# Decode block on one Trainium2 core: how the late chunk of the down projection is loaded, and where the passes wait

## Chip, cores, metric

One core of one Trainium2 chip runs the whole program. The metric is device time in microseconds, the median of several runs. All data are float32.

## What is computed

A decode step for 8 tokens of width 1024: layer norm, attention with 32 query heads over the last 1024 positions of a cache with 4 key/value heads, output projection and residual; then layer norm, a gated feed-forward of width 3584 and residual.

```python
h = x + attention(layernorm(x), k_cache, v_cache, wq, wo)
n = layernorm(h)
out = h + (gelu(n @ w_gate) * (n @ w_up)) @ w_down      # (8,1024) @ (1024,3584), (3584,1024)
```

The weights and the cache window come to 111 MB, and each is used once.

## The kernel before, in words

**Passes.** The work is seven passes over one PE loop body (`products`, L479): 0 query projection, 1 scores, 2 attention times V, 3 output projection (`WO`), 4 and 5 gate and up columns (`GU0`, `GU1`), 6 the down projection (`DN`). A pass has a side a on buffer `buf[0]` and a side b on `buf[1]`; pass 6 has side a only. A side is eight steps of four matmuls (the profile counts two records for each), whose 32-row results stand in the four quarters of the partitions of `ob`. A full side's load is 8192 KB.

**Waits.** Every place at which PE may have to wait is a name in a fixed order (`pe_order`, L118): for side a of pass k the steps 0 (`a{k}`), CUTS[1] (`a{k}m`) and CUTS[2] (`a{k}l`), with CUTS = (0, 4, 7, 8). `need` (L294 to L419) says which semaphores stand behind a name. GpSimd goes through the names in order (L450 to L457), waits for what a name needs (L455) or for nothing (L457), and counts `go` up by one; PE waits for `go` (L462) and counts it down. So PE learns of a landed load through GpSimd.

**Loads.** SP issues all loads, in order, through `move` (L108): the sides of passes 0 to 4 whole, those of pass 5 in halves of 4096 KB (L187 on), each as soon as PE has left the buffer. Pass 6 has the rows of w_down in pieces: 8 chunks of 128 rows came along with pass 5, 16 chunks are its eight steps (three loads of 4096, 3072 and 1024 KB by CUTS, L194, into `buf[0]`), and four late chunks go to `buf[1]`, free when side b of pass 5 is done. The first late chunk, `singles[0]` of 512 KB (128 rows of 4 KB), is loaded in three pieces of 32, 88 and 8 rows (ROWCUTS, L202 and L203); two more singles of 512 KB and two end blocks of 256 KB follow (L208 and L214). Behind them SP issues 15 `tag` loads (L219) of 15, 14, ... 1 rows with some 100 bytes each, whose data nothing uses; SP waits for them at L441, after it has issued its half of the store.

**The tail on PE.** Steps 0 to 3, 4 to 6 and 7 of pass 6 wait for the three main loads. In two places of pass 6 and one of pass 5 PE repeats an earlier matmul on `fin` (AGAIN, `repeat_residual`, L475; without use for the result). Then come the late chunks: `singles[0]` with two matmuls into quarters 0 and 2 of `ob[0]` (L530), the singles into `fin` (L524), the fold of the sums `d1` that DVE adds up (L426), and the two end blocks (L541), each followed by an ACT copy (L430) and its half of the store, one issued by SP and one by ACT.

Side a of pass 5 starts on its first half as soon as that lands; the second half is awaited at step 4 (L416). In pass 6 step 0 awaits the first main load and ACT's copy `first_ok`, step 4 the second load and ACT's `late_ok` (L417, L418; both copies spread the activations over `st[0]`, L379).

Of the kernel before, what the change touches and what calls it, by code (L numbers as in the profile page):

```python
# [8 lines left out]
P = 128  # L9
B = 8  # L10
D = 1024
# [5 lines left out]
NQ = 4  # L17
CP = 32 // B
QW = D // NQ
N = 512  # L20
# [4 lines left out]
STEPS = 8  # L25
LOAD = STEPS * NQ * N
PASSES = 7
WO, GU0, GU1, DN = 3, 4, 5, 6
CUTS = (0, 4, 7, STEPS)
LAST = DF // P - 1  # L30
EARLY = 8
ENDS = (128, 128)
SINGLE = 3
ROWCUTS = (0, 32, 120, P)
TAGS = 15
AGAIN = (((0, DN, 2), (STEPS // 2, DN, 2)), ((STEPS // 2, GU1, 4),))


class Flow:
# [57 lines left out]
    def run(self, engine, make, *waits, mark=True):  # L97
        ins = self.start(engine, make, waits)
        if not mark:
            return None  # L100
        self.done[engine] += 1
        ins.then_inc(self.own[engine], 1)
        self.tell(engine, self.own[engine], self.done[engine])
        return self.own[engine], self.done[engine]

    def move(self, name, out, src, *waits, engine="sync"):
        s = self.sem(name)
        self.start(engine, lambda e: e.dma_start(out, src), waits).then_inc(s, 16)  # L108
        self.tell(engine, s, 16)
        return s, 16  # L110
# [19 lines left out]
    return out  # L130


def decode_block(nc, x, w, dn, single, ends, outs):
    fl = Flow(nc)
    run, move = fl.run, fl.move
    scale = DH ** -0.5
# [2 lines left out]
    need = {}  # L139
# [30 lines left out]
    ob = [bank(f"o{i}", 2 * N) for i in range(2)]  # L170
# [3 lines left out]
    go = fl.sem("go")  # L174
# [23 lines left out]
    for i in range(SINGLE):  # L198
        t = buf[1][:, i * D:(i + 1) * D]
        if i == 0:  # L200
            here = fl.sem("ws0")
            for a, b in zip(ROWCUTS, ROWCUTS[1:]):  # L202
                fl.start("sync", lambda e: e.dma_start(t[a:b], single[i][a:b]), [pe(f"b{GU1}")]).then_inc(  # L203
                    here, 16)
            here = here, 16 * (len(ROWCUTS) - 1)
        else:
            here = move(f"ws{i}", t, single[i])
        singles.append((t, here))  # L208
    blocks = []
    c0 = 0  # L210
    for i, (n, src) in enumerate(zip(ENDS, ends)):
        a = SINGLE * D + NQ * c0
        t = buf[1][:, a:a + NQ * n]
        blocks.append((n, t, move(f"we{i}", t, src)))  # L214
        c0 += n
# [71 lines left out]
    st_ok = [(t,) for t in tokens_in([pe("t")])]  # L287
    tt_free = st_ok[0]
    o_free = [(), ()]
# [81 lines left out]
    at = sb("at", P, DF // P, 32)  # L371
    ge, g0, u0, u1 = (sb(n, P, N) for n in ("ge", "g0", "u0", "u1"))
    lent = [t.rearrange("p (i r m) -> p i r m", i=STEPS, r=NQ)[:, :, NQ - 1, :] for t in st]
    wide = st[0].rearrange("p (i c m) -> p i c m", i=STEPS, c=2)

    def widen(i0, i1, *ready):

        src = at[:, EARLY + 2 * i0:EARLY + 2 * i1].rearrange("p (i e) m -> p i (e m)", e=2)
        return run("scalar", lambda e: e.copy(  # L379
            wide[:, i0:i1], src.unsqueeze(2).to_broadcast([P, i1 - i0, 2, 64])), *ready)  # L380
# [40 lines left out]

# [10 lines left out]
    mark = sb("mark", 1, 1)  # L432
# [14 lines left out]
        nc.sync.wait_ge(s, val).then_inc(s, -val)  # L447


    for name in [n for kind, n in order if kind == "wait"]:  # L450
        left = fl.missing("gpsimd", need.get(name, []))
        for s, v in left[:-1]:
            nc.gpsimd.wait_ge(s, v)
        if left:
            nc.gpsimd.wait_ge(*left[-1]).then_inc(go, 1)  # L455
        else:
            nc.gpsimd.sem_inc(go, 1)  # L457
    assert set(need) <= {n for kind, n in order if kind == "wait"}, need


# [35 lines left out]
    with nc.Fori(-1, PASSES, engines=[mybir.EngineType.PE]) as it:  # L496
        with nc.tensor.If(it >= 0):
            wait()
            turn(xs[1])
            products(0, CUTS)  # L500
            with nc.tensor.If(it < DN):
# [3 lines left out]
                with nc.tensor.If(it == WO):  # L505
                    wait()
                    for ch in range(2):
                        ins = nc.tensor.matmul(
                            fin[0:ROWS, ch * N:(ch + 1) * N], to_rows[:, ch, :], y_sb,
                            start=True, stop=True)  # L510
                    marked(ins)
                    wait()
                    for ch in range(2):
# [3 lines left out]
                            start=True, stop=True)  # L517
                    marked(ins)

    def add(lhs, rhs, *waits, start=False):  # L520

        for d_ps, a, b in halves:
            for j in range(NQ):
                run("tensor", lambda e: e.matmul(  # L524
                    d_ps[32 * j:32 * j + 32, :], lhs(j), rhs(j)[:, a:b], start=start, stop=False),
                    *waits, mark=False)

    (t, here), *rest = singles
    for ch in range(2):
        tok = run("tensor", lambda e: e.matmul(  # L530
            ob[0][64 * ch:64 * ch + 32, N:2 * N], at[:, LAST - SINGLE, :], t[:, ch * N:(ch + 1) * N],
            start=False, stop=True, skip_group_check=True), here, at_ok, mark=(ch == 1))
    assert tok == odd_done
    for i, (t, here) in enumerate(rest):
        add(lambda j: at[:, LAST - SINGLE + 1 + i, :], lambda j: t[:, j * QW:(j + 1) * QW], here,
            start=(i == 0))
        if i == 0:
            add(lambda j: add2[:, j // 2, :], lambda j: d1[:, (j % 2) * QW:(j % 2) * QW + QW], d1_ok)
    for (n, t, here), (d_ps, a, b) in zip(blocks, halves):
        for j in range(NQ):  # L540
            run("tensor", lambda e: e.matmul(  # L541
                d_ps[32 * j:32 * j + 32, :], at[:, LAST, :], t[:, j * n:(j + 1) * n],
                start=False, stop=True), here, mark=(j == NQ - 1))
# [65 lines left out]
```

## Time and profile before

| | |
|---|---|
| median of 3 runs | 268.08 us (267.64 to 270.53) |
| the profiled execution | 267.8 us, its span 266.2 us |
| mean granted TensorE clock | 0.833 |
| read from HBM | 111.19 MB, 418 GB/s over the span |
| PE busy | 145.5 us (55%) |
| VectorE, ScalarE, GpSimd busy | 28.6, 28.5, 5.3 us |

How to read it. The span runs from the first to the last instruction of the program; the program's own time is somewhat longer. A row of the timeline gives the start, the length, engine and line, the operation with its tiles, the count and, in brackets, how long the engine had been idle and what ended that. "SPq", "PEq" and "POOLq" are the sequencers' own instructions (issues of loads, waits). A row by stage has each engine's busy time (and its instructions) within that stretch, then the granted clock, the busy share of the 16 DMA engines (a packet is put down to the stretch in which it starts, so 1.03 can occur) and what they moved. In the DMA answer for a stretch, "packets" counts rows of data and the 4-byte notices at a load's end ("under 512 B").

### The profile page before, as it was taken

How to read it: one execution, taken by the hardware profiler on the slowest of the kernel's cores; microseconds unless marked ns; L12 is line 12 of the kernel's file. 1: busy time of each engine (PE TensorE's matmuls, PEld its weight loads, DVE VectorE, ACT ScalarE, POOL GpSimd, SP SyncE). 2: the span in 40 equal slices, each digit the busy share in tenths (PEclk: the TensorE clock that was granted, in tenths of full speed). 3: DMA queues.
4: the chain of work that ended last, by engine and by line, in shares of the span. 5: the costliest groups of instructions: out<-in, count | busy, mean ns of one | idle time of the engine just before them, and what ended most of it. 6: DMA issues, size and time to landing. Idle time of an engine off the chain costs nothing. (4 is left out here: it accounts for less than half of the span.)

```text
span 266.2 us, 2425 instructions
## 1 busy us (share of the span) xinstructions
PE 145.5 (55%) x1028; PEld 50.3 (19%) x1028; DVE 28.6 (11%) x47; ACT 28.5 (11%) x49; POOL 5.3 (2%) x11
## 2 busy tenths in 40 slices
PE   0023924815716727518519609638829564886784
PEld 0021211201211222102102202122202221322222
DVE  0310020100100100500500101430100201002101
ACT  1030000020030030010010000033300102002000
POOL 8000000000000000000000000000000000000000
PEclk9999995975975956966965968975977999799979
DMA  8997999799979997999799979997999999999994
GB/s 318 468 473 325 473 463 473 325 473 463 473 325 473 463 473 325 473 463 473 325 473 463 473 335 463 463 473 335 463 394 468 394 473 394 473 394 435 420 274 164
DMA packets 3735, 111.38 MB, mean 418 GB/s; under 512 B 651, under 2 KB 907, under 8 KB 1555
## 3 DMA queue, kind: packets, MB, share of 16 engines
q1 hardware_dynamic: 3571, 111.23, 98.0%
q10 hardware_dynamic: 160, 0.10, 0.1%
q8 instruction: 2, 0.03, 0.0%
q14 instruction: 2, 0.02, 0.0%
HBM read 111.19 MB, written 0.13 MB: 418 GB/s over the span
## 5 line engine op out<-in xcount | busy, mean ns | idle before, releaser
L489 PE MATMUL o<-w,st 128*32 128x512 f32 x832 | 116.3, 717 | 79.0 <-PEq L462 47.4
L489 PEld LDWEIGHTS o<-w,st 128*32 128x32 f32 x832 | 32.8, 129 | 154.9 <-issue 154.9
L469 PE MATMUL tt<-ident,zeros 128*128 128x128 f32 x104 | 16.5, 311 | 35.8 <-PEq L462 35.8
L469 PEld LDWEIGHTS tt<-ident,zeros 128*128 128x128 f32 x104 | 13.3, 159 | 46.2 <-issue 46.2
L475 PE MATMUL fin<-zeros,spread 128*32 128x512 f32 x16 | 7.4, 594 | 0.0
L331 DVE SCALAR_TENSOR_TENSOR av<-o,rtot,own 128x512 f32<-128x512 f32 x4 | 3.0, 750 | 31.3 <-PE o L489 31.3
L314 DVE TENSOR_REDUCE nmax<-o 128x1 f32<-128x1024 f32 x2 | 2.5, 1225 | 35.3 <-PE o L489 35.3
L341 ACT COPY st<-tt 128x512 f32<-128x512 f32 x4 | 2.1, 588 | 35.4 <-PE tt L469 35.4
L316 ACT ACTIVATE zeros<-o,nmax 128x1024 f32<-128x1024 f32 x2 | 2.2, 1114 | 33.6 <-DVE nmax L314 33.6
L356 DVE TENSOR_TENSOR y_sb<-o,y_sb 128x512 f32<-128x512 f32 x3 | 2.1, 692 | 34.2 <-PE o L489 34.2
L296 DVE SCALAR_TENSOR_TENSOR zeros<-o,tq 128x512 f32<-128x512 f32 x2 | 1.4, 692 | 36.1 <-PE o L489 36.1
L399 DVE TENSOR_TENSOR u<-o,u 128x512 f32<-128x512 f32 x2 | 1.4, 692 | 35.1 <-PE o L489 35.1
L390 DVE TENSOR_TENSOR g<-o,g 128x512 f32<-128x512 f32 x2 | 1.4, 692 | 24.6 <-PE o L489 24.6
L295 ACT ACTIVATE tq<-o 128x512 f32<-128x512 f32 x2 | 1.2, 597 | 24.0 <-PE o L489 24.0
L334 DVE TENSOR_REDUCE zeros<-av 128x128 f32<-128x1024 f32 x2 | 3.7, 1871 | 0.1
L398 ACT COPY u<-o 128x512 f32<-128x512 f32 x2 | 1.2, 586 | 21.0 <-PE o L489 21.0
L363 ACT COPY zeros<-fin 32x512 f32<-32x512 f32 x1 | 0.6, 574 | 26.4 <-PE fin L514 26.4
L227 POOL MEMSET zeros<- 128x3712 f32 x1 | 3.2, 3191 | 0.0
L263 ACT ACT_TABLE_LOAD x2 | 2.6, 1283 | 2.9 <-POOL ident L224 2.9
L279 ACT COPY st<-tt 128x1024 f32<-128x1024 f32 x2 | 2.0, 1012 | 7.7 <-PE tt L469 7.7
L405 ACT COPY at<-tt 128x512 f32<-128x512 f32 (+1 forms) x2 | 1.1, 532 | 16.0 <-PE tt L469 16.0
L475 PEld LDWEIGHTS fin<-zeros,spread 128*32 128x32 f32 x16 | 1.7, 110 | 4.5 <-issue 4.5
(57 smaller groups left out, 40.9 us busy)
## 6 DMA issues: line engine op xcount, KB each, us to landing
w<-ends SPq DMA_DIRECT2D x5, 4096.0 KB, 25.3
w<-ends SPq DMA_DIRECT2D x1, 3072.0 KB, 32.2
w<-ends SPq DMA_DIRECT2D x1, 1024.0 KB, 36.2
w<-ends SPq DMA_DIRECT2D x2, 512.0 KB, 18.7
w<-ends SPq DMA_DIRECT2D x2, 256.0 KB, 19.5
w<-ends SPq DMA_DIRECT2D x1, 352.0 KB
w<-w SPq DMA_DIRECT2D x10, 29.5
w<-ends SPq DMA_DIRECT2D x1, 128.0 KB
```

The costliest lines, as they stand in the source:

```text
L227: clear = run("gpsimd", lambda e: e.memset(zeros, 0.0))
L263: tok = run("scalar", lambda e: e.activation(sd, ve, AF.Sqrt), tok)
L279: a = run("scalar", lambda e: e.copy(st[0].rearrange("p (c r b) -> p c r b", c=NC, b=B), xt.unsqueeze(2).to_broadcast([P, NC, P // B, B])) ...
L314: tok = run("vector", lambda e: e.tensor_reduce(out=nmax, in_=ob[s], axis=AX.X, op=ALU.max, negate=True), pe(f"{h}1"))
L316: tok = run("scalar", lambda e: e.activation(xs[s], ob[s], AF.Exp, bias=nmax, accum_out=tot), tok)
L331: tok = run("vector", lambda e: e.scalar_tensor_tensor(av[:, i], o3, rtot, own.unsqueeze(2).to_broadcast([P, HB, DH]), op0=ALU.mult, op1=A ...
L334: tok = run("vector", lambda e: e.tensor_reduce(out=out, in_=av.rearrange("p i b d -> p d (i b)"), axis=AX.X, op=ALU.add), tok)
L341: tok = run("scalar", lambda e: e.copy(heads[:, g], turned.unsqueeze(2).to_broadcast([P, REP, P // 2 // B, B])), pe(f"t{h}2"))
L356: tok = run("vector", lambda e: e.tensor_add(y_sb, part, y_sb), ready, tok)
L469: ins = nc.tensor.transpose(t8[:, i, :], src[:, i * P:(i + 1) * P], ident)
L475: nc.tensor.matmul(fin[0:32, 0:N], spread.rearrange("p r b -> p (r b)"), h_sb[:, 0:N], start=True, stop=True)
L489: ins = nc.tensor.matmul(ob[s][32 * r:32 * r + 32, c:c + N], st[s][:, i * P + 32 * r:i * P + 32 * r + 32], buf[s][:, (i * NQ + r) * N:(i * ...
```

## The change

1. The first late chunk is laid out anew on the host. Its columns 0 to 511 stay as 128 rows of 2 KB (`w_odd`, one load through `move`). Its columns 512 to 1023 become 64 rows of 4 KB on partitions 0 to 63 (`w_low`): row p has the half row of partition p and, behind it, that of partition p + 64. Eight loads of eight rows bring them; load j writes partitions p0, p0 + 4, ... p0 + 28 with p0 from OFFSETS. The matmuls on the chunk are three: all 128 rows into quarter 0, and two with 64 rows into quarters 2 and 3 (the fold adds both). For the last one ACT copies the upper 64 partitions of the activations down (`at_low`).
2. CUTS becomes (0, 5, 7, 8): the main loads are 5120, 2048 and 1024 KB, and PE's middle wait stands at step 5. Both halves of pass 5's side a are now awaited at step 0, and `late_ok` at step 0 of pass 6. The second repeat of pass 6 moves to step 5.
3. GpSimd no longer takes a step of its own for a name without needs: the wait before it counts `go` up by as many as follow it.

```diff
-CUTS = (0, 4, 7, STEPS)
+CUTS = (0, 5, 7, STEPS)
-ROWCUTS = (0, 32, 120, P)
+LOW = P // 2
+OFFSETS = (0, 1, 2, 3, 32, 33, 34, 35)
-AGAIN = (((0, DN, 2), (STEPS // 2, DN, 2)), ((STEPS // 2, GU1, 4),))
+AGAIN = (((0, DN, 2), (CUTS[1], DN, 2)), ((STEPS // 2, GU1, 4),))
...
+    w_odd, w_low = buf[1][:, 0:N], buf[1][0:LOW, N:N + D]
+    odd_in = [move("wo0", w_odd, single[0], pe(f"b{GU1}"))]
+    low_in = fl.sem("w_low")
+    for j, p0 in enumerate(OFFSETS):
+        nc.sync.dma_start(w_low[p0:p0 + 29:4], side[j]).then_inc(low_in, 16)
+    odd_in.append((low_in, 16 * len(OFFSETS)))
-        if i == 0:
-            here = fl.sem("ws0")
-            for a, b in zip(ROWCUTS, ROWCUTS[1:]):
-                fl.start("sync", lambda e: e.dma_start(t[a:b], single[i][a:b]), [pe(f"b{GU1}")]).then_inc(
-                    here, 16)
...
-        need[f"a{k}"] = [landed[k, 0][0], *st_ok[0], *o_free[0]]
+        need[f"a{k}"] = [*landed[k, 0], *st_ok[0], *o_free[0]]
...
+            low_ok = run("scalar", lambda e: e.copy(at_low, at[LOW:P, LAST - SINGLE, :]), at_ok)
-    need[f"a{GU1}m"] = [*landed[GU1, 0][1:], res_ok]
-    need[f"a{DN}"] = [landed[DN, 0][0], first_ok, *o_free[0]]
-    need[f"a{DN}m"] = [landed[DN, 0][1], late_ok]
+    need[f"a{GU1}m"] = [res_ok]
+    need[f"a{DN}"] = [landed[DN, 0][0], first_ok, late_ok, *o_free[0]]
+    need[f"a{DN}m"] = [landed[DN, 0][1]]
...
+    steps = []
     for name in [n for kind, n in order if kind == "wait"]:
         left = fl.missing("gpsimd", need.get(name, []))
+        if left or not steps:
+            steps.append([left, 1])
+        else:
+            steps[-1][1] += 1
+    for left, n in steps:
         for s, v in left[:-1]:
             nc.gpsimd.wait_ge(s, v)
-        if left:
-            nc.gpsimd.wait_ge(*left[-1]).then_inc(go, 1)
-        else:
-            nc.gpsimd.sem_inc(go, 1)
+        nc.gpsimd.wait_ge(*left[-1]).then_inc(go, n)
...
-    for ch in range(2):
+    odd = LAST - SINGLE
+    for i, (q, lhs, t) in enumerate((
+            (0, at[:, odd, :], w_odd), (2, at[0:LOW, odd, :], w_low[:, 0:N]),
+            (3, at_low, w_low[:, N:2 * N]))):
         tok = run("tensor", lambda e: e.matmul(
-            ob[0][64 * ch:64 * ch + 32, N:2 * N], at[:, LAST - SINGLE, :], t[:, ch * N:(ch + 1) * N],
-            start=False, stop=True, skip_group_check=True), here, at_ok, mark=(ch == 1))
+            ob[0][32 * q:32 * q + 32, N:2 * N], lhs, t, start=False, stop=True,
+            skip_group_check=True), *odd_in, at_ok, low_ok, mark=(i == 2))
...
+    low = odd[:, 1].reshape(2, LOW, N).transpose(1, 0, 2)
+    parts += [np.stack([low[p0:p0 + 29:4] for p0 in OFFSETS]), odd[:, 0]]
```

More of the change, by code (lines that the diff above doesn't have):

```diff
@@ L130, in pe_order, with decode_block @@
     return out
-def decode_block(nc, x, w, dn, single, ends, outs):
+def decode_block(nc, x, w, dn, side, single, ends, outs):
     fl = Flow(nc)
@@ L196, in decode_block @@
         for i, (a, b) in enumerate(zip(CUTS, CUTS[1:]))]
-    singles = []
-    for i in range(SINGLE):
-        t = buf[1][:, i * D:(i + 1) * D]
-        if i == 0:
-            here = fl.sem("ws0")
-            for a, b in zip(ROWCUTS, ROWCUTS[1:]):
-                fl.start("sync", lambda e: e.dma_start(t[a:b], single[i][a:b]), [pe(f"b{GU1}")]).then_inc(
-                    here, 16)
-            here = here, 16 * (len(ROWCUTS) - 1)
-        else:
-            here = move(f"ws{i}", t, single[i])
-        singles.append((t, here))
+    w_odd, w_low = buf[1][:, 0:N], buf[1][0:LOW, N:N + D]
[4 more added lines that the diff above has]
+    odd_in.append((low_in, 16 * len(OFFSETS)))
+    singles = []
+    for i in range(1, SINGLE):
+        t = buf[1][:, N + i * D:N + (i + 1) * D]
+        singles.append((t, move(f"ws{i}", t, single[i])))
     blocks = []
@@ L211, in decode_block @@
     for i, (n, src) in enumerate(zip(ENDS, ends)):
-        a = SINGLE * D + NQ * c0
+        a = N + SINGLE * D + NQ * c0
         t = buf[1][:, a:a + NQ * n]
@@ L373, in decode_block @@
     lent = [t.rearrange("p (i r m) -> p i r m", i=STEPS, r=NQ)[:, :, NQ - 1, :] for t in st]
+    at_low = sb("at_low", LOW, 32)
     wide = st[0].rearrange("p (i c m) -> p i c m", i=STEPS, c=2)
@@ L447, in decode_block @@
         nc.sync.wait_ge(s, val).then_inc(s, -val)
+    steps = []
     for name in [n for kind, n in order if kind == "wait"]:
         left = fl.missing("gpsimd", need.get(name, []))
+        if left or not steps:
[3 more added lines that the diff above has]
+    for left, n in steps:
         for s, v in left[:-1]:
             nc.gpsimd.wait_ge(s, v)
-        if left:
-            nc.gpsimd.wait_ge(*left[-1]).then_inc(go, 1)
-        else:
-            nc.gpsimd.sem_inc(go, 1)
+        nc.gpsimd.wait_ge(*left[-1]).then_inc(go, n)
     assert set(need) <= {n for kind, n in order if kind == "wait"}, need
@@ L526, in add @@
                     *waits, mark=False)
-    (t, here), *rest = singles
-    for ch in range(2):
+    odd = LAST - SINGLE
+    for i, (q, lhs, t) in enumerate((
+            (0, at[:, odd, :], w_odd), (2, at[0:LOW, odd, :], w_low[:, 0:N]),
+            (3, at_low, w_low[:, N:2 * N]))):
         tok = run("tensor", lambda e: e.matmul(
-            ob[0][64 * ch:64 * ch + 32, N:2 * N], at[:, LAST - SINGLE, :], t[:, ch * N:(ch + 1) * N],
-            start=False, stop=True, skip_group_check=True), here, at_ok, mark=(ch == 1))
+            ob[0][32 * q:32 * q + 32, N:2 * N], lhs, t, start=False, stop=True,
+            skip_group_check=True), *odd_in, at_ok, low_ok, mark=(i == 2))
     assert tok == odd_done
-    for i, (t, here) in enumerate(rest):
-        add(lambda j: at[:, LAST - SINGLE + 1 + i, :], lambda j: t[:, j * QW:(j + 1) * QW], here,
+    for i, (t, here) in enumerate(singles):
+        add(lambda j: at[:, odd + 1 + i, :], lambda j: t[:, j * QW:(j + 1) * QW], here,
             start=(i == 0))
@@ L579 @@
     parts += [main[:, a * NQ:b * NQ] for a, b in zip(CUTS, CUTS[1:])]
-    parts += [down[:, i] for i in range(LAST - SINGLE, LAST)]
+    odd = down[:, LAST - SINGLE]
+    low = odd[:, 1].reshape(2, LOW, N).transpose(1, 0, 2)
+    parts += [np.stack([low[p0:p0 + 29:4] for p0 in OFFSETS]), odd[:, 0]]
+    parts += [down[:, i] for i in range(LAST - SINGLE + 1, LAST)]
     parts += [row[:, :, a:b] for a, b in zip(cuts, cuts[1:])]
@@ L600 @@
     w = [aps["w"][i] for i in range(2 * GU1)] + small[0:4]
-    dn, single, ends = small[4:7], small[7:7 + SINGLE], small[7 + SINGLE:]
-    decode_block(nc, aps["x"], w, dn, single, ends, outs)
+    dn, side, single, ends = small[4:7], small[7], small[8:8 + SINGLE], small[8 + SINGLE:]
+    side = side.rearrange("p n -> (p n)").rearrange("(j r n) -> j r n", j=len(OFFSETS), r=8)
+    decode_block(nc, aps["x"], w, dn, side, single, ends, outs)
     r = run_bass_kernel_spmd(nc, [arrays], core_ids=[0])
```

## The prediction

> **What bounds the kernel now.** I read the page first, then the chain that ended last, then busy time by stage, then the DMA answer for short stretches of the tail, then the timeline of the last 20 us.
>
> ```profile
> span 266.2 us, 2425 instructions
> PE 145.5 (55%) x1028; PEld 50.3 (19%) x1028; DVE 28.6 (11%) x47; ACT 28.5 (11%) x49; POOL 5.3 (2%) x11
> q1 hardware_dynamic: 3571, 111.23, 98.0%
> ...
> 243.35 19.61 DMA w<-ends
> ...
> 263.01 0.47 PE fin L541 x8
> ...
> 263.50 0.27 ACT o_fin L430
> ```
>
> SP's queue keeps the 16 DMA engines taken for 98.0% of the span, and the chain ends with one load of 19.61 us that lands at 262.96 (243.35 + 19.61); then 0.47 us of PE, 0.27 us of ACT and the store follow. So the kernel ends when the last of its loads lands. The program took 267.8 us with this profile, 1.6 us more than its span; the median of the runs shown is 268.08 us, 0.28 more. My sum is a difference of spans, taken off that median.
>
> A busy DMA engine is not a fast one, and the stages show it:
>
> ```profile
> core 0: us, PE busy (x) PEld busy (x) DVE busy (x) ACT busy (x) POOL busy (x), PEclk, DMA share, GB/s
> 237.00:246.80 9.80, 6.54 (x44) 2.34 (x44) 1.39 (x2) 1.71 (x3) 0.00 (x0) 1.00 1.02 440
> 254.10:258.60 4.50, 4.44 (x24) 1.27 (x24) 0.00 (x0) 0.00 (x0) 0.00 (x0) 0.62 1.03 223
> 258.60:263.00 4.40, 3.69 (x71) 1.88 (x68) 0.75 (x2) 0.23 (x1) 0.00 (x0) 1.00 0.80 291
> ```
>
> While the first part of the main down rows is loaded, the engines are full at 440 GB/s. From 254.10 to 258.60 they are just as full (1.03) and move 223. That stretch holds the three row pieces of the late chunk. Had it run at 440, it would have been (1 - 223/440) x 4.50 = 2.2 us shorter. The same in two shorter stretches, the pieces first, then the ordinary 4 KB rows behind them:
>
> ```profile
> DMA packets 151, 0.52 MB, mean 187 GB/s; under 512 B 25, under 2 KB 25, under 8 KB 149
> q1 hardware_dynamic: 151, 0.52, 104.3%
> ...
> DMA packets 182, 0.56 MB, mean 402 GB/s; under 512 B 20, under 2 KB 20, under 8 KB 182
> q1 hardware_dynamic: 182, 0.56, 101.9%
> ```
>
> Between 255.60 and 258.40 a row of some 4 KB holds its engine for 2.80 x 16 x 1.043 / 126 = 0.37 us; between 259.20 and 260.60 one of the same kind takes 1.40 x 16 x 1.019 / 162 = 0.14 us. By engine these are 187/1.043/16 = 11.2 GB/s and 402/1.019/16 = 24.7 GB/s. Row size and busy engines are alike; what differs is which partitions an engine writes. I read it as engines standing in each other's way at the SBUF side: with 88 rows over fewer engines than 16, each takes a block of rows that other engines write too.
>
> **The change part by part.** *The late chunk's loads.* Its 512 KB move as one load of 128 rows of 2 KB (spread as the other full loads) and eight loads of 8 rows of 4 KB, whose rows stand four partitions apart, one row for each of eight engines. So eight engines carry 16 + 32 KB of the chunk, the others 16 KB. To time an engine I need when it begins the third main load:
>
> ```profile
> DMA packets 61, 0.49 MB, mean 410 GB/s; under 512 B 1, under 2 KB 1, under 8 KB 1
> q1 hardware_dynamic: 61, 0.49, 98.3%
> ...
> 254.16 5.54 PE L489 MATMUL o<-w,st 128*32 128x512 f32 x32 [1.98 <-PEq L462]
> ```
>
> Between 252.75 and 253.95, 60 rows of 8 KB (0.49 MB / 60) begin: they are the third main load's. All 16 engines at 440/1.02/16 = 27.0 GB/s would begin 63, so about 15 of them are past the second load at 252.75, yet PE gets that load only at 254.1: one engine is some 1.4 us behind. I put the others at 252.6 (half a row earlier), the late one at 254.0. Each then has, by rates of 27.0 (8 KB rows) and 24.7 (smaller): third main load 64 KB 2.43 us, the 2 KB rows 0.66, its eight 4 KB rows 1.33 (eight engines only), the two single chunks 2.65, the two end blocks 1.33. That is 8.40 us for the eight, 7.07 for the rest. The eight finish at 261.0, with 0.2 for the telling 261.2. The late engine, if it is among the rest, finishes at 254.0 + 7.07 = 261.1. Against 262.96 the last landing is **1.8 us** earlier.
>
> The price of a small load beyond its bytes has no row of its own. Nearest are the fifteen tag loads behind the last block:
>
> ```profile
> SPq L441 <- DMA tag<-w: 2.2, 1, 2.2
> L219 SPq DMA_DIRECT2D tag<-w x15: 252/329/2694, 243.8 to 253.7; - x15
> ...
> 240.84 1.12 SPq L203 DMA_DIRECT2D w<-ends  x3
> 242.01 1.78 SPq L108 DMA_DIRECT2D w<-ends  x4
> 243.83 10.15 SPq L219 DMA_DIRECT2D tag<-w  x15
> 263.13 0.37 SPq L108 DMA_DIRECT2D out<-o_fin  x1
> ```
>
> SP waits for them from 263.50 (263.13 + 0.37) for 2.2 us, to about 265.7: 2.8 us after the last block, 0.19 each. Eight such prices are 1.5 us; below, nothing, and no gain. I take nothing: between 259.20 and 260.60 twenty 4-byte notices passed among 162 rows at 24.7 GB/s. The Trainium skill's page "DMA: Bandwidth & Descriptors" speaks against the change: its "Rules for kernel authors" would have small transfers gathered, since under 64 KB one pays mostly overhead. Its table of measured sizes (0.68 us for 4 KB, 0.95 for 64 KB) would make eight loads cost about 6.4 us as an estimate, and the sum would turn into a loss of some 3 us.
>
> *SP's queue.* Six more issues at 0.37 to 0.45 us (1.12/3, 1.78/4) are 2.2 to 2.7 us; the fifteen tags behind them would end at 254 + 2.7 = 256.7, and should SP be held up again as in the 2.7 us issue above, at 259.4. The store's turn comes at 261.3, so 1.9 us of cover are left; the loads themselves wait behind a full queue.
>
> *Cuts at 5 and 7, the second half of pass 5's load, late copies.* The step 0 wait now covers both halves of that load:
>
> ```profile
> 211.91 3.64 PE L489 MATMUL o<-w,st 128*32 128x512 f32 x32 [1.28 <-PEq L462]
> ...
> 217.74 3.64 PE L489 MATMUL o<-w,st 128*32 128x512 f32 x32 [2.18 <-POOLq L457]
> ...
> 227.44 5.24 PE L489 MATMUL o<-w,st 128*32 128x512 f32 x32 [5.04 <-PEq L462]
> 232.43 3.60 PE L475 MATMUL fin<-zeros,spread 128*32 128x512 f32 x8
> 237.16 3.64 PE L489 MATMUL o<-w,st 128*32 128x512 f32 x32 [1.12 <-PEq L462]
> ...
> 244.15 0.62 ACT L379 COPY st<-at 128x512 f32<-128x512 f32 x1
> ```
>
> The 3.64 us at 211.91 move behind 217.74, so that half ends at 225.0 and its turn in time for the next load at 227.4: nothing. Behind the longer wait GpSimd has only the same pass's later increments, which PE alone awaits. At half clock throughout, the half would end at 232.3, and what follows (5.24 + 3.60 us) at some 241 where PE goes on at 237.16 now: 4 us late. Then the late copies, ready at 244.8 (244.15 + 0.62) and now awaited at step 0 of the last pass, would come at 249, when that step's load lands, and the late chunk would be issued at 245, ten microseconds ahead of its turn. So hidden even then, with little to spare.
>
> In the last pass the first part holds five steps, 1 MB more at 440 GB/s, and lands at 246.8 + 2.4 = 249.2. What PE then has to do, from rows of before:
>
> ```profile
> 246.87 3.64 PE L489 MATMUL o<-w,st 128*32 128x512 f32 x32 [1.43 <-PEq L462]
> 250.30 1.88 PE L475 MATMUL fin<-zeros,spread 128*32 128x512 f32 x4
> 259.49 1.06 PE L530 MATMUL o<-w,at 128*32 128x512 f32 x4
> 260.66 0.69 DVE L426 TENSOR_TENSOR d<-o,d 128x512 f32<-128x512 f32 x1 [9.33 <-PE o L530]
> 261.41 0.64 PE L524 MATMUL fin<-d,add 128*32 128x128 f32 x16 [0.42 <-DVE d L426]
> 261.87 0.62 PE L524 MATMUL fin<-w,at 128*32 128x128 f32 x16
> 262.31 0.40 PE L541 MATMUL fin<-w,at 128*32 128x128 f32 x8
> 263.01 0.43 PE L541 MATMUL fin<-w,at 128*32 128x128 f32 x8 [0.30 <-DMA w<-ends]
> ```
>
> From start to start 32 matmul records take 3.43 us (246.87 to 250.30). Five steps take 4.3, to 253.5; the repeats, moved to step 5, 1.7, to 255.3 (the second part landed at 254.1, so they delay it by 1.1); two steps 1.7, to 257.0; the last 0.9, to 257.9. The chunk is there at 257.2. Three matmuls stand in place of two; the two ran side by side in 1.06 us, and I let the third do so (between 0 and 0.5 us more). The DVE add starts 1.17 later, the fold 0.75, the last single 0.46, the first end block 0.44: 260.7. The last block lands at 261.2, so PE has half a microsecond in hand. The new copy of 64 partitions is one ACT instruction of about 0.6 us at 246 or so, 10 us ahead of its use.
>
> *Fewer GpSimd waits.*
>
> ```profile
> L457 POOLq EVENT_SEMAPHORE  x18: 17/17/17, 24.0 to 217.7; - x18
> ```
>
> Eighteen bare increments of 17 ns go. All stand beside loads that are on their way; worth nothing, 0.3 us (18 x 17 ns) at the very most.
>
> **Sum.** Last landing -1.8 us; PE, SP and GpSimd 0; the 3.2 us from landing to end (262.96 to 266.2) as before. 268.08 - 1.8 = **266.3 us**.
>
> **The rivals.** *PE takes over the end.* The granted clock was 0.62 from 254.10 to 258.60, after PE had idled 1.98 us. Half clock in one stretch of 3.4 us (a half pass of 32 records) costs 1.7 us of work. The first end block's work would start at 262.4, the last one's at 262.8 where before had 263.01: -0.2, **267.9 us**. For it: half a microsecond of slack. Against: the repeats now fill the gap that cooled PE. The Trainium skill's "TensorE: Matmul & The Clock Gate", Part 1, says that the activity window runs freely, so that the place of the drop may vary; no single trace can show that.
>
> *The late engine is among the eight, or stepped rows clash as well.* The page does not tell which engine is late. It would end at 254.0 + 8.40 = 262.4: -0.6, **267.5 us**. For: the eight carry more. Against: before ended with a DMA share of 0.80 from 258.60 on, so several engines had run out early, and those had the two rows only.
>
> *Small loads hold their engines (slower).* If each of the eight costs a fixed time in series, the chunk and all behind it come later. From 1.8/8 = 0.22 us a load the gain is gone; at SP's own issue price, 0.45, it is 8 x 0.45 - 1.8 = 1.8 us lost, **269.9 us**, and from 0.56 over 1%; the far end is a store's whole way, 2.4 us (below), and 17 us lost. For: the tags' 0.19 is close to the turning point. Against: the notices seen above hold nothing up.
>
> *More than the clash goes.* With all rows at 27.0 GB/s the eight have 208 KB, 7.9 us, and end at 260.7: -2.3; if the store, 2.4 us from issue to landing now, also finds the queue free of tags and lands 0.7 earlier, **265.1 us**.
>
> ```profile
> out<-o_fin ACTq DMA_DIRECT2D x1, 64.0 KB, 2.4
> ```
>
> **How the numbers follow.** Forecast 0.60, PE 0.15, late engine or clash 0.10, small loads 0.07, more 0.08. The range 265.2 to 268.4 runs from just above the last rival over 267.9 to a small-load price near the tags' 0.19 with a little PE on top; it leaves out the small-load rival and most of the last one, some 0.15. About 1% (2.7 us) is what a measurement of this kernel can tell from no change. Faster by more needs 265.4: the last rival and a sliver of the forecast, 0.10. Slower by more needs 270.8: most of the small-load rival, 0.05. Within: 0.85.
>
> **What would show it.** Right: 254 to 258 at well over 300 GB/s where 223 stood; 4 KB rows at 0.14 to 0.17 us throughout; the last block's matmuls at about 261.3; PE there waiting for DMA. Wrong: rows still at 0.37 us (clash); the odd chunk's matmuls after 259 with PE idle before them (small loads); the last block's matmuls directly behind other PE work at half clock (PE); an SP issue of tags that reaches past 261.

## The result, and the profile after

| | before | changed |
|---|---|---|
| median | 268.00 us (20 runs, 267.49 to 270.71) | **267.37 us** (20 runs, 265.66 to 268.04) |
| ratio to before, with its 95% interval | | 0.9943 [0.9917, 0.9968] |
| the profiled execution | 267.8 us, span 266.2 | 265.81 us, span 264.5 |

The change is a gain of half a per cent, inside what the forecast called no change, and inside its range. But the median hides the more useful fact. The 20 runs of the changed kernel lie in two groups with nothing between them: seven from 265.66 to 265.95 and thirteen from 267.19 to 268.04. The profiled execution belongs to the first. Disturbed runs are left out of every ratio here.

The page of the changed kernel (span, and the chain that ended last by engine and by line). Line numbers have moved: the products are L493, the repeats L479, the late chunk L536, singles and fold L528, end blocks L547.

```profile
span 264.5 us, 2418 instructions
...
PE 5%; DVE 0%; ACT 0%; issue 0%; DVEq 0%
PE o L493 3%; PE o L536 1%; PE fin L479 1%; PE fin L528 0%; DVE d L427 0%; ACT o_fin L431 0%; PE fin L547 0%; DVE mark L434 0%; DVEq L92 0%
```

The chain no longer has a load in it. It was one load of 19.61 us; now it is PE from the start of the last pass on. Busy time by stage, with the stretch 254.10 to 258.60 that the forecast argued from:

```profile
237.00:249.20 12.20, 8.23 (x44) 2.80 (x44) 1.38 (x2) 1.93 (x4) 0.00 (x0) 0.86 0.94 405
249.20:254.10 4.90, 4.74 (x42) 1.68 (x43) 0.69 (x1) 0.00 (x0) 0.00 (x0) 1.00 0.97 408
254.10:258.60 4.50, 4.50 (x30) 1.24 (x28) 0.00 (x0) 0.00 (x0) 0.00 (x0) 1.00 1.01 396
258.60:261.30 2.70, 2.41 (x41) 1.01 (x44) 0.69 (x2) 0.00 (x0) 0.00 (x0) 1.00 0.55 192
```

396 GB/s stand where 223 stood, at the same full engines, and from 258.60 to 261.30 the engines are already half idle (0.55). The DMA answers for 255.5 to 257.5, where the eight small loads are under way, for the issue of the last end block, and for the store:

```profile
DMA packets 268, 0.82 MB, mean 408 GB/s; under 512 B 66, under 2 KB 66, under 8 KB 267
q1 hardware_dynamic: 268, 0.82, 103.0%
...
w<-ends SPq DMA_DIRECT2D x1, 256.0 KB, 11.3
...
out<-o_fin ACTq DMA_DIRECT2D x1, 64.0 KB, 1.8
```

There are 268 - 66 = 202 rows in 2.0 us, nearly all of 4 KB (0.82 MB / 202): the stepped rows and those of the single chunks behind them. So a 4 KB row takes 2.0 x 16 x 1.03 / 202 = **0.163 us** where it took 0.37. The store took 1.8 us from issue to landing where it took 2.4. The timeline of the end:

```profile
243.00 5.45 SPq L202 DMA_DIRECT2D w<-ends  x8
...
249.36 4.50 PE L493 MATMUL o<-w,st 128*32 128x512 f32 x40 [2.14 <-PEq L466]
...
249.93 0.43 SPq L109 DMA_DIRECT2D w<-ends  x1
250.40 5.65 SPq L218 DMA_DIRECT2D tag<-w  x15
253.65 1.45 PE L479 MATMUL fin<-zeros,spread 128*32 128x512 f32 x3
...
257.94 1.56 PE L536 MATMUL o<-w,at 128*32 128x512 f32 x3
258.89 0.10 PEld L536 LDWEIGHTS o<-w,at 64*32 64x32 f32 x1 [0.84 <-issue]
258.90 0.61 PE L536 MATMUL o<-w,at_low 64*32 64x512 f32 x1
...
260.06 0.69 DVE L427 TENSOR_TENSOR d<-o,d 128x512 f32<-128x512 f32 x1 [6.24 <-PE o L536]
...
261.70 0.62 PE L547 MATMUL fin<-w,at 128*32 128x128 f32 x16
262.69 0.35 ACTq L109 DMA_DIRECT2D out<-o_fin  x1
```

The last end block, issued at 249.93, landed 11.3 us later, at **261.2**. PE reached its 16 matmul records at 261.70, both blocks in one go and with no wait in front: the data had been there for half a microsecond. PE ends the kernel.

### The profile page after: what moved, and what is told of

The parts are those of the page before. It is cut to its first block, busy times and chain, and to the rows that moved or that the text cites. A ratio compares the mean times of both kernels' runs of the same rounds, so it can differ in the third digit from the quotient of the medians.

```text
span 264.5 us, 2418 instructions
## 1 busy us (share of the span) xinstructions
PE 147.1 (56%) x1030; PEld 50.4 (19%) x1030; DVE 28.5 (11%) x47; ACT 28.7 (11%) x50; POOL 5.3 (2%) x11
## 5 line engine op out<-in xcount | busy, mean ns | idle before, releaser
L493 PE MATMUL o<-w,st 128*32 128x512 f32 x832 | 118.0, 725 | 76.5 <-PEq L466 70.1
L493 PEld LDWEIGHTS o<-w,st 128*32 128x32 f32 x832 | 33.0, 130 | 153.0 <-issue 152.9
L479 PE MATMUL fin<-zeros,spread 128*32 128x512 f32 x16 | 7.4, 594 | 0.0
L389 ACT COPY g<-o 128x512 f32<-128x512 f32 x2 | 1.2, 586 | 16.2 <-PE o L493 16.2
## 6 DMA issues: line engine op xcount, KB each, us to landing
w<-ends SPq DMA_DIRECT2D x3, 256.0 KB, 11.3
```

What stands on the lines that cost most here:

```text
L479: nc.tensor.matmul(fin[0:32, 0:N], spread.rearrange("p r b -> p (r b)"), h_sb[:, 0:N], start=True, stop=True)
L493: ins = nc.tensor.matmul(ob[s][32 * r:32 * r + 32, c:c + N], st[s][:, i * P + 32 * r:i * P + 32 * r + 32], buf[s][:, (i * NQ + r) * N:(i * ...
```

## Experiments

**What was to be told apart.** Theory: the new loads bring the last landing from 263.0 to 261.2 and nothing else in the change gains; PE, now last, decides the rest, and the second group of runs is PE at half clock in the last pass. Rivals: the cuts or the GpSimd part bring the gain; the stepped rows are not what ends the clash; small loads have a price that eight of them already pay; the second group has another cause.

**1. The changed kernel again.** No edit.

> The changed kernel once more, unaltered, for its spread and a second profile. Its runs fall in two groups, near 265.8 and near 267.5 us. Theory (PE's clock): the last block has landed at about 261.2 in both groups; in the slower one the main steps of the last pass run at half clock for one stretch and all PE work behind them comes 1.7 us later, so that the last end block's matmuls start near 263.6 with their data long there. Rival (the loads): in the slower group the last block itself lands 1.7 us later, near 263, and PE waits for it.

Measured: 267.39 us median of 12 runs, 0.9962 [0.9944, 0.998]; ten runs lie from 267.11 on, two at 266.44 and 266.63, between the two groups. This time the profile (267.39 us, span 266.1) was of the slower group. Its timeline and the stage 249.20 to 254.10:

```profile
237.29 3.64 PE L493 MATMUL o<-w,st 128*32 128x512 f32 x32 [2.32 <-PEq L466]
...
248.28 0.43 SPq L109 DMA_DIRECT2D w<-ends  x1
249.41 6.07 PE L493 MATMUL o<-w,st 128*32 128x512 f32 x40 [3.84 <-PEq L466]
...
259.58 1.56 PE L536 MATMUL o<-w,at 128*32 128x512 f32 x3
...
263.34 0.62 PE L547 MATMUL fin<-w,at 128*32 128x128 f32 x16
```

```profile
249.20:254.10 4.90, 4.69 (x32) 1.42 (x36) 0.00 (x0) 0.00 (x0) 0.00 (x0) 0.65 0.97 411
...
w<-ends SPq DMA_DIRECT2D x1, 256.0 KB, 12.9
```

The last block landed at 248.28 + 12.9 = 261.2, as before. But the five steps from 249.41 took 6.07 us, not 4.50, at a granted clock of 0.65, not 1.00; everything behind is 1.64 us later (259.58 against 257.94, 263.34 against 261.70), and so is the span (266.1 against 264.5). Both profiles have one stretch of half clock near the end, 3.4 us long by the clock's records. In the first it ran from 237.8 to 241.2, on the half pass before (a mean clock of 0.86 from 237.00 to 249.20), which has time to spare. In the second that half pass ran warm in 3.64 us, PE was done sooner and idled 3.84 us, not 2.14, and the half clock ran from 249.2 to 252.6, in the last pass, where nothing is spare. That the longer idle time brought it there is argued, not shown: experiment 9 has it there after 2.13 us. The forecast took from the Trainium skill ("TensorE: Matmul & The Clock Gate", Part 1) that the activity window runs freely and the place of the drop may vary; these two profiles of one program agree, with 0.65 and 1.00 in the same stage.

**2 to 4. The parts alone.** Kernel before with part 2 alone (cuts and waits); with parts 1 and 3 (loads, GpSimd, the old cuts); with part 3 alone. Of each its first line:

```diff
+CUTS = (0, 5, 7, STEPS)
...
+OFFSETS = (0, 1, 2, 3, 32, 33, 34, 35)
...
+        nc.gpsimd.wait_ge(*left[-1]).then_inc(go, n)
```

> The kernel before with only the cuts at 5 and 7, the waits that go with them and the moved repeat; loads of the late chunk and GpSimd's steps as before. Theory (the loads bring the gain): last landing at 263.0 as before, time 268.0, ratio 1.000. Rival (the cuts bring some of it): ratio below 0.998. PE's slack before the last block was 0.3 us; should the half clock fall on it, up to 0.5 us slower.

> The new layout and loads of the late chunk with the old cuts, waits and repeats (GpSimd's merged steps stay). Theory (loads give, PE takes): the last block lands at about 261.2 as with the full change; the half clock after the idle gap before step 4, as in the profile of before, makes the chunk's matmuls start near 259.4 and the last block's near 263.2: time 267.2 to 267.6, ratio 0.998. Rival (the landing decides): 266.2, ratio 0.993.

> The kernel before with only GpSimd's merged steps. Theory: nothing, ratio 1.000 within the interval, last landing at 263.0. Rival (PE waited for the bare increments on the path that sets the end): 0.1 to 0.3 us faster.

| kernel | median us | ratio, 95% interval |
|---|---|---|
| cuts alone | 268.55 (12 runs) | 1.0002 [0.9982, 1.0022] |
| loads and GpSimd, old cuts | 267.03 (12 runs) | 0.9944 [0.9918, 0.9971] |
| GpSimd alone | 267.81 (10 runs) | 0.9991 [0.9957, 1.0025] |

The chain of the cuts alone, then of GpSimd alone, then the stage of the loads alone:

```profile
243.45 19.95 DMA w<-ends
```

```profile
243.44 19.60 DMA w<-ends
```

```profile
254.10:258.60 4.50, 4.48 (x28) 1.57 (x32) 0.00 (x0) 0.00 (x0) 0.00 (x0) 0.64 1.02 402
```

Without the new loads the last block still lands at 263.4 and 263.0 and ends the kernel. With them the stretch moves 402 GB/s. So the loads bring the whole gain; the cuts and the fewer GpSimd steps bring nothing that can be measured. The loads alone have the two groups as well (four of the 12 runs at 265.9 to 266.1), and in their profile, 267.17 us, the half clock (0.64) fell on 254.10 to 258.60, as expected; their median is a little under the 267.2 to 267.6 expected of it.

**5. PE kept busy where it may cool, and free where it is late.** The repeats at step 5 go, seven are put ahead of side a of pass 5, and four, not two, ahead of the last pass. The repeats are not used by the result.

```diff
-AGAIN = (((0, DN, 2), (CUTS[1], DN, 2)), ((STEPS // 2, GU1, 4),))
+AGAIN = (((0, GU1, 7), (0, DN, 4)), ((STEPS // 2, GU1, 4),))
```

> The change with other repeats: seven more before side a of pass 5, four in place of two before step 0 of the last pass, none at step 5, so that PE has no idle stretch of several us before its last work. Theory (PE's clock): one group, all near 265.8 us, ratio 0.992 to before; granted clock 1.00 from 249 on. Rival (the two groups come from the loads): still two groups, median near 267.4, ratio 0.995 to 0.997.

Measured: 266.15 us median of 8 runs, 0.9921 [0.9896, 0.9946]; of the seven that the ratio counts, six lie at or under 266.43 and one at 267.23. Timeline and landing:

```profile
249.99 0.43 SPq L109 DMA_DIRECT2D w<-ends  x1
...
257.76 1.56 PE L536 MATMUL o<-w,at 128*32 128x512 f32 x3
...
261.52 0.62 PE L547 MATMUL fin<-w,at 128*32 128x128 f32 x16
```

```profile
w<-ends SPq DMA_DIRECT2D x1, 256.0 KB, 11.2
```

The landing is untouched (249.99 + 11.2 = 261.2), and so is the rate while the small loads are under way (408 GB/s from 255.5 to 257.5). PE's end is only 0.18 earlier than in the changed kernel's first profile, and the clock is 1.00 from 249.20 on. The median falls by 1.2 us (267.39 to 266.15), so PE has a part in the second group. But the edit does two things, and it is not shown that the clock is the one that counts: of the later profiles with the same repeats, those of experiments 7, 8 and 9 have half clock (0.65) from 249.20 to 254.10 all the same. Here are the row and the timeline of 9, whose loads are those of this experiment:

```profile
249.20:254.10 4.90, 4.49 (x28) 1.59 (x32) 0.00 (x0) 0.00 (x0) 0.00 (x0) 0.65 0.99 416
...
249.61 8.77 PE L493 MATMUL o<-w,st 128*32 128x512 f32 x64 [2.13 <-PEq L466]
258.17 1.56 PE L536 MATMUL o<-w,at 128*32 128x512 f32 x3
```

PE begins the chunk at 258.17, 0.41 us after 257.76, where the same half clock cost 1.64 us in experiment 1. Without the repeats at step 5 PE's eight steps run through in one go, and most of the half clock is made up before the chunk is there. So at least part of the gain comes from the repeats that went, not from a clock that stayed up.

**6 to 8. What the eight stepped loads avoid, and what they cost.** All three have the repeats of experiment 5, which is what they are compared with (by the ratios, for they ran on another chip and beside other runs of the kernel before: a median of 267.94 us there, 268.05 for experiment 5). 6: the same eight loads, on eight consecutive partitions each. 7: the 64 rows in one load. 8: sixteen loads of eight rows of 2 KB.

```diff
-        nc.sync.dma_start(w_low[p0:p0 + 29:4], side[j]).then_inc(low_in, 16)
+        nc.sync.dma_start(w_low[8 * j:8 * j + 8], side[j]).then_inc(low_in, 16)
...
+    nc.sync.dma_start(w_low, side).then_inc(low_in, 16)
...
+        for h in range(2):
+            nc.sync.dma_start(w_low[p0:p0 + 29:4, h * N:h * N + N], side[2 * j + h]).then_inc(low_in, 16)
```

> The change with its repeats as in the run called warm, and one thing else: each of the eight small loads writes eight partitions in a row (8j to 8j+7) and not eight that stand four apart. Number, size and engines of the loads stay. Theory (the rows' partitions decide, since engines stand in each other's way): rows of 4 KB hold their engines 0.3 us and more, as in the three pieces before, and the chunk lands late. If a group of four partitions takes no more than one engine's 27 GB/s, eight rows over two groups need 0.6 us, the eight loads 4.8 in place of 1.3: last landing 264.7, time 269.3. Rival (number and kind of the loads decide): last landing at 261.2 as in warm, time 265.8 to 266.2.

> As warm, but the lower section's 64 rows come in one load. By the Trainium skill's count it spreads over 16 engines, four rows each. Theory (clash): 16 engines write the places of eight, so a row takes 0.32 us, four rows 1.3 us on every engine, and the late engine, spared in the change, ends at about 262.5: time 267.1. Rival (no clash, small loads were the cost): 0.16 us a row, the late engine ends at 261.8 and the others at 260.4, time 266.4.

> As warm, but each of the eight small loads is cut into two of 8 rows of 2 KB: 16 loads, on the same engines and partitions. Theory (a load costs its engines no more than its bytes): last landing 261.2 to 261.3, time as warm. Rival (each small load holds its engines some 0.19 us): eight more are 1.5 us, last landing 262.7, time 267.3. SP's eight more issues of some 0.6 us are 5 us, which its queue can bear; should it not, the tags end after 261 and the store comes late.

| kernel | median us (10 runs each) | ratio, 95% interval | last block issued + to landing |
|---|---|---|---|
| 5, eight stepped loads | 266.15 (8 runs) | 0.9921 [0.9896, 0.9946] | 249.99 + 11.2 = 261.2 |
| 6, consecutive rows | 266.89 | 0.9954 [0.9936, 0.9972] | 247.29 + 14.6 = 261.9 |
| 7, one load | 267.41 | 0.9978 [0.9943, 1.0012] | 243.43 + 19.5 = 262.9 |
| 8, sixteen loads | 267.43 | 0.9993 [0.9966, 1.002] | 253.64 + 8.6 = 262.2 |

The DMA answers for 255.5 to 257.5, first of kernel 6, then of 7 (with PE's row where it begins the chunk):

```profile
DMA packets 199, 0.54 MB, mean 268 GB/s; under 512 B 63, under 2 KB 63, under 8 KB 197
q1 hardware_dynamic: 199, 0.54, 102.5%
...
w<-ends SPq DMA_DIRECT2D x1, 256.0 KB, 14.6
```

```profile
DMA packets 129, 0.45 MB, mean 226 GB/s; under 512 B 16, under 2 KB 16, under 8 KB 128
q1 hardware_dynamic: 129, 0.45, 97.6%
...
259.49 1.56 PE L535 MATMUL o<-w,at 128*32 128x512 f32 x3 [0.84 <-DMA w<-ends]
...
w<-ends SPq DMA_DIRECT2D x1, 256.0 KB, 19.5
```

A 4 KB row takes 2.0 x 16 x 1.025 / 136 = 0.24 us on consecutive partitions and 2.0 x 16 x 0.976 / 113 = 0.28 us in one load, against 0.163 stepped. The bytes and the engines' share of time are the same. In 6 the number and size of the loads are the same too; only which partitions an engine writes differs. That is the clash the forecast inferred, shown by putting it back. In 7 the number of loads and of engines changes as well, so it agrees without being as clean. In the one load it costs 1.7 us of landing and nearly the whole gain, about as expected. PE was at half clock in the last pass there, but it stood idle for 0.84 us until the chunk landed, so the load decides and not PE. On consecutive partitions it costs 0.7 us, far less than I expected of it. My guess is that the engines do not run in step, so that rows of several loads are under way at once and meet only in part; no run shows that.

Of the sixteen loads, the timeline and the landing, then the DMA answers for 256.6 to 258.6, first of kernel 8, then of 5:

```profile
253.64 0.43 SPq L109 DMA_DIRECT2D w<-ends  x1
...
259.27 1.56 PE L537 MATMUL o<-w,at 128*32 128x512 f32 x3 [1.07 <-DMA w<-ends]
```

```profile
w<-ends SPq DMA_DIRECT2D x1, 256.0 KB, 8.6
...
DMA packets 223, 0.65 MB, mean 327 GB/s; under 512 B 25, under 2 KB 25, under 8 KB 223
...
DMA packets 263, 0.81 MB, mean 406 GB/s; under 512 B 32, under 2 KB 32, under 8 KB 263
```

PE waits for the chunk here and gets it 1.5 us later than in experiment 5 (259.27 against 257.76), the last block lands 1.0 us later, for the same bytes. Eight more loads therefore cost 1.0/8 to 1.5/8, **0.13 to 0.19 us each**, one behind another. The rows are half as long too (2 KB), and no run changes the number of loads alone.

The landing records of the traces speak for the loads: with one row for each of eight engines, the sixteen loads report from 255.76 to 259.13, 3.37/16 = 0.21 us for each, and the eight of experiment 5 from 255.81 to 257.63, 1.82/8 = 0.23 us, though a row of 2 KB takes some 0.085 us and one of 4 KB 0.163; the last tags of the kernel before reported 0.17 to 0.20 us apart. So small loads behind one another report some 0.2 us apart here, whatever their rows. At eight loads with 4 KB rows most of that is the row's own time, and the landing of 261.2 is what the sum gives with no price at all. The reading that fits is that an engine pays the longer of the row and the notice at its end, one beside the other; that part is argued, not shown.

In kernel 8 the engines' share from 256.6 to 258.6 is the same as in 5 (102.0 and 102.5%) at 327 GB/s against 406, so the time shows up as longer rows behind the small loads. The small-transfer rule of the Trainium skill ("DMA: Bandwidth & Descriptors", Rules for kernel authors), priced by the page's table (section Bandwidth, Measured, for loads issued from GpSimd), made eight loads cost 6.4 us as an estimate; loads that SP queues one behind another do not bear that out, at some 0.2 us each.

**9. PE's own tail shortened.** On top of experiment 5: the matmul with 128 rows waits for its own load alone, and the fold comes after the second single chunk, so that PE has work while DVE adds.

```diff
-            skip_group_check=True), *odd_in, at_ok, low_ok, mark=(i == 2))
+            skip_group_check=True), *(odd_in[1:] + [low_ok] if i else odd_in[:1]), at_ok, mark=(i == 2))
...
-        if i == 0:
+        if i == 1:
```

> As warm, with less PE work behind the late chunk: the matmul on the 128-row section waits for its own load alone and so runs before the lower section lands, and the fold of the sums comes after the second single, not before it. Theory (with the clock kept up, PE's chain behind the late chunk ends last, 0.6 us after the last landing): PE ends with the last landing, 0.6 us sooner, time 265.2 to 265.5, ratio 0.990 to 0.991 to before. Rival (the landing or the store's way decides already): as warm, 265.8 to 266.2.

Measured: 266.01 us median of 10 runs, 0.9915 [0.9884, 0.9945]: seven runs at 265.74 to 266.12 and three at 267.42 to 267.50. The profile is of one of the three, and it is not PE: in spite of the half clock shown under experiment 5 the last matmuls start at 261.50, before those of the first profile above, and the store is issued at 262.56. The DMA answer for 263.2 to 264.9, and that store's way:

```profile
DMA packets 270, 0.14 MB, mean 82 GB/s; under 512 B 30, under 2 KB 269, under 8 KB 269
...
q8 instruction: 1, 0.02, 6.0%
...
out<-o_fin ACTq DMA_DIRECT2D x1, 64.0 KB, 3.5
```

The store took 3.5 us, not 1.8. In the same moment one packet of 16 KB on the queue "instruction", by its name a load of program code, holds one engine for 0.060 x 16 x 1.7 = 1.63 us. By the records 15 engines' shares of the two stores had landed by 264.64; the 16th, behind that packet, at 266.06.

**10. PE kept at full clock for good.** Six repeats where experiment 5 has four.

```diff
-AGAIN = (((0, GU1, 7), (0, DN, 4)), ((STEPS // 2, GU1, 4),))
+AGAIN = (((0, GU1, 7), (0, DN, 6)), ((STEPS // 2, GU1, 6),))
```

> The change with more repeats than in warm: seven before side a of pass 5, six at step 4 of its side b, six before step 0 of the last pass, none at step 5. In two profiles with four repeats the clock was halved all the same, at 249.7 and 250.0, after PE had idled 2.1 us. Theory (PE's clock makes the two groups): no half clock from 204 to the end, one group near 265.8 us, ratio 0.991 to 0.992. Rival (something else makes the groups): runs near 267.4 remain in number.

Measured: 266.52 us median of 10 runs, 0.9938 [0.9907, 0.9969]: five runs at 265.70 to 265.93, five at 267.10 to 267.36. The profile is of the first five and has a clock of 1.00 in every stage quoted above. The one group that the theory asked for did not come. The mean clock of the other five, 0.833 to 0.846, is no lower than that of the first (0.832 to 0.845), but a mean over the whole program does not say in which stage the clock was halved. Half clock in the last pass cost 0.41 us with four repeats (experiment 9); the second group is some 1.2 us away. So the clock hardly makes the whole of the second group here, though no profile shows what does.

**11 and 12. Without the tag loads.** 11 is experiment 10 without the fifteen loads whose data nothing uses, and without SP's wait for them; 12 is 9 and 11 together.

```diff
-    for k in range(TAGS, 0, -1):
-        nc.sync.dma_start(tag[0:k, k - 1, 0:16 + k], w[0][0:k, 0:16 + k]).then_inc(tags, 16)
...
-    nc.sync.wait_ge(tags, 16 * TAGS)
```

> As steady, without the fifteen tag loads (their data is used nowhere) and SP's wait for them. Theory (behind an earlier last landing the tags' notices and the store's way hold the end): the stores land as soon as they are written; span 0.2 to 0.4 us shorter, 265.4 to 265.6. Rival (PE's end and the store's way alone set it): as steady, 265.8.

> As steady, with PE's chain behind the late chunk shortened as in sooner and without the tags. Theory (in sooner the 0.6 us that PE gained were lost to the tags' notices and, in its profile, to a 16 KB code load of 1.64 us on the instruction queue that held one engine's store): 0.6 us below steady without tags where the code load does not meet the store, 264.9 to 265.1; where it does, up to 1.4 us later, so possibly two groups. Rival (the last landing decides): as steady without tags.

Measured: 11 has 265.55 us, four runs from 265.42 to 265.63, 0.989 [0.9836, 0.9943]; that is what the theory said (its span is 264.3 us against 264.5), and it is the lowest median here, below that of both kernels, though four runs are too few to say that it has no second group. 12 has 266.58 us, ten runs from 265.19 to 267.02, 0.9915 [0.9885, 0.9944]. The store's way in 11, then the timeline and the DMA answers of 12 (262.2 to 264.9, then its last part from 263.2 on):

```profile
out<-o_fin ACTq DMA_DIRECT2D x1, 64.0 KB, 1.7
```

```profile
260.90 0.62 PE L542 MATMUL fin<-w,at 128*32 128x128 f32 x16
...
261.88 0.36 ACTq L109 DMA_DIRECT2D out<-o_fin  x1
```

```profile
q8 instruction: 1, 0.02, 3.8%
...
out<-o_fin ACTq DMA_DIRECT2D x1, 64.0 KB, 3.6
...
DMA packets 16, 0.01 MB, mean 5 GB/s; under 512 B 1, under 2 KB 16, under 8 KB 16
```

Kernel 12 has PE done 0.7 us sooner than 11 (260.90 against 261.59) and ends 1.2 us later (span 265.5 against 264.3). Its store meets the code load, 0.038 x 16 x 2.7 = 1.64 us on one engine, and from 263.2 on only sixteen packets trickle in, at 5 GB/s, while 15 engines are done. A store that is ready sooner is not safer here: in 12 it was issued 0.7 us before that of 11 and met the code load. Nor is the code load's time fixed: in 9 the store was issued about when those of 10 and 11 were, and the code load came at 263.23, where 10 has it at 261.81. What sets that is not known. In the profiles where the store took 1.7 or 1.8 us, the code load was over, or nearly, when the store's first rows moved (262.04 plus 1.20 against 263.40 in the changed kernel).

## Why the prediction was right, point by point

- **Last landing 1.8 us earlier, at 261.2.** Right to a tenth, and for its reason: 4 KB rows at 0.163 us (forecast 0.14 to 0.17), over 300 GB/s from 254 to 258, and the clash comes back when the rows are put together again (experiments 6 and 7). The assumption that the late engine is among the eight that carry less is borne out: by the landing records seven engines have their share of the last block at 259.4 to 259.8 and nine at 260.8 to 261.2. Two slips in the working did no harm. The 0.14 us is a mean over 4 KB rows and shorter ones (0.56 MB in 162 rows is 3.5 KB each); the sum used the rate, 24.7 GB/s, by which a 4 KB row takes 0.17. And the 0.2 us for the telling was not added for the late engine, which makes 261.3.
- **PE has half a microsecond in hand.** This step failed. PE was half a microsecond behind the landing. The steps up to the chunk came as worked out (257.9 forecast, 257.94 measured), the repeats at step 5 delaying them as the working said. The mis-sized term is "three matmuls stand in place of two", with 0 to 0.5 us: the add started 2.12 us after the chunk's first matmul (260.06 - 257.94), not 1.17. The two matmuls with 64 rows do run side by side, but only once the one with 128 rows is through (258.90, with 0.84 us of idle weight loading before it). The term is **0.95 us**.
- **The tail from landing to end, 3.2 us.** It measured 3.3 (261.2 to 264.5), by luck: two errors cancel. 0.5 us of PE were added, and the store took 1.8 us, not 2.4, as the rival "more than the clash goes" had it.
- **SP six more issues, 2.2 to 2.7 us.** Mis-sized: the eight took 5.45 us, 0.68 each, where three pieces took 1.12. Still nothing, since the cover held: the last tag was issued by 256.05 (250.40 + 5.65), six microseconds ahead of the store.
- **Small loads nothing.** Right for eight with 4 KB rows, and not a rule: sixteen with 2 KB rows pay 0.13 to 0.19 us for each one more, close to the tags' 0.19 that the forecast named and set aside.
- **Cuts and GpSimd nothing.** Right (1.0002 and 0.9991, both intervals hold 1).
- **The rival "PE takes over the end", 267.9 us.** Its chance of 0.15 was too low. In the profile of 267.39 us (experiment 1) it is there with its mechanism and nearly its price (1.64 us, against 1.7 worked out); the group near that time holds 13 of 20 runs, of which none was profiled. The ground against it, that the repeats fill the gap that cooled PE, failed: the cooling moved to the idle time ahead of the last pass. So the median, 267.37, is not the forecast's case of 266.3: that lies between the two groups. The lowest runs of the two kernels, 265.66 and 267.49, are 1.83 us apart, the forecast's own term; but that term comes out whole only because the PE and store errors cancel, so the agreement is partly luck.

**What stays open.** Two causes of a slower run are in the profiles, half clock in the last pass (experiments 1 and 3) and a store caught by the code load (9 and 12). Which of them makes each of the unprofiled runs is not known, above all the five of experiment 10, whose mean clock was no lower. Kernel before also spreads, from 267.49 to 270.71, and was not taken apart. A simpler change was not tried: the late chunk in one plain load of 128 rows of 4 KB, as the singles have it, with the two matmuls kept. By the forecast's own terms its last landing would be 254.0 + 2.43 + 1.33 + 2.65 + 1.33 + 0.2 = 261.9 us, an estimate: 0.7 later than the stepped loads, but without the 0.95 us on PE. So it is shown that taking the clash away brings the gain, not that the stepped layout is the best way to do it.

## What to carry to other kernels

When a share of busy DMA engines stays at 1 and the rate halves, look at which partitions each engine writes, and lay the rows out so that concurrent engines write apart; the gain is then computable from rows of the same trace. Count the loads too: sixteen small ones gave the same sign (327 GB/s at a full share). Before booking it, time what ends next as closely as what ends now, matmul by matmul: a shape that changes from 128 to 64 rows may not overlap its neighbour. Where the medians differ by less than the spread, list the runs: two groups say that the end hangs on something that varies from run to run, and one profile shows only one of them.

## What the runs showed of the hardware

- A matmul with 64 rows did not start beside one with 128 rows into another quarter, in every profile of the changed kernel: 0.96 us from one's start to the other's. In the kernel before, two with 128 rows in quarters 0 and 2 ran in 1.06 us together.
- An SP issue of a load with eight rows four partitions apart took 0.68 us (5.45/8), on eight consecutive partitions 0.34 (2.73/8, experiment 6), that of a whole block 0.43.
- Small loads queued behind one another reported some 0.2 us apart, with rows of 4 KB, of 2 KB and of some 100 bytes alike (experiments 5 and 8, and the tags of the kernel before).
- Near the end of the program a 16 KB load on the queue "instruction" took one DMA engine for 0.96 us (experiment 10) to 1.64 us (experiment 12), and a store whose rows queue behind it on that engine landed 1.7 to 1.9 us later (3.5 and 3.6 us, not 1.7 and 1.8).
